# A rest product on 128 rows, and the next weights' preparation laid out over two units

## The chip, the cores and the metric

The kernel runs on one core of a Trainium2 chip. The metric is device time in microseconds (us). Before the change three runs took 1530.38, 1531.14 and 1531.47 us; their median is 1531.14 us.

## The reference

An attention block of the mLSTM kind feeds a mixture of eight experts. The attention output `x` has 3072 rows and 320 columns. The experts are dense: all of them see every row, and a matrix of weights P, made from gate logits by eight rounds of row and column normalisation, adds them up:

```python
for e in range(E):                      # E = 8
    h = np.maximum(x @ w1[e], 0.0)      # 320 -> 1024
    ye = h @ w2[e]                      # 1024 -> 320
    out += P[:, e:e + 1] * ye
```

All is in float32. The change lies in the experts 2 to 7 alone.

## The kernel before, in words

The attention and the experts 0 and 1 come first, up to about 537 us of the profiled execution. Then comes the part that the change touches. It takes the experts e = 2 to 7, the 1024 hidden columns of each in four pairs of 128-column blocks (g = 0 to 3), and the 3072 rows of x in three parts (p = 0 to 2). A *group* is one (e, g), 24 in all; a *unit* is one (e, g, p), 72 in all.

Precision. Each float32 operand is split into a high part, rounded to the type that TensorE takes (fp32r), and a low part, the remainder. ScalarE makes the high part by a copy, GpSimd or VectorE the low part by a subtraction. A product is then high x high, high x low and low x high.

A unit (`Fast.unit`, line 299) computes the two blocks of `x @ w1` for two halves of its rows by seven block products in place of eight (a Strassen-like scheme). Each product (`Fast.product`, lines 269 to 282) is four matmuls of 512 columns. Three, line 280, treat 128 of x's columns on 128 rows. The fourth, line 282, treats the "rest": x has 320 columns, and what remains of them beside 256 is stacked on 96 rows (high, low and high again, each HR = 32 rows), against three stacked pieces of the weights. The stacked x lies in DRAM (`xr`) and is loaded for every product by `rest_load` into one of twelve places in `xt` (`rest_slot`), which hold no other data by then.

The results leave PSUM in three ways: line 330 (ScalarE copies the first product), line 315 (VectorE adds a product to `tp`), and `h_parts`, which applies the ReLU and splits the hidden values: line 326 (ScalarE, high) with line 327 (VectorE, low) for the first half, and lines 322, 323 (ScalarE) with 324 (GpSimd, low) for the second. One of the two calls of line 327 in a unit reads `tp`, so both of its operands lie in SBUF; the other reads PSUM.

`Fast.second` (lines 284 to 297) multiplies the hidden values by w2: 24 matmuls of 320 columns for each half, line 297. The first half's run stands at the end of its unit, the second half's at slot 4 of the next unit. Line 158 (VectorE) adds the result into `acc`, weighted by P.

While a group is computed, the weights of the next group are prepared (`prep`, lines 1001 to 1005): `w_load` (lines 232 to 243) loads w1 and w2 in nine DMAs from SP's queue into `st` and `st2`; `w_sums` (line 248) forms four sums of blocks, in four instructions on GpSimd; `w_split` splits the main part (lines 263, 264), the rest (265, 266) and w2 (256, 257), ScalarE first and GpSimd after it. The results go into one of two sets of places, by turns of groups. There are 23 preparations inside the units, and one before them.

The order of the work is written out by hand: `at(slot, fn)` puts a piece at a slot, and the pieces are issued in the order of their slots, so a slot sets only the order on each engine and queue, not a time. A unit is 9 slots. Products stand at the slots 0 to 3 and 5 to 7, line 326 on `tp` behind slot 5.6, lines 322 to 324 at 7.7 and 7.8, the first half's second matmuls at 8. In the old plan the preparation stands in unit p = 1: the load at slot 0.9, the sums at 4.0, the splits at 5.0 and 5.1. The `rest_load` of a product is planned 9 slots before it; it waits until the product that held its place twelve products ago is done.

Of the kernel before, what the change touches and what calls it, by code (L numbers as in the profile page):

```python
# [16 lines left out]
def f32(ap):  # L17
    return ap.bitcast(F32)
# [3 lines left out]
def mlstm_moe_kernel(ctx, tc, q, k, v, i_gate, f_gate, o_gate, moe_w_gate, moe_w1, moe_w2, out):  # L22
    nc = tc.nc
# [23 lines left out]
    xt = big.tile([128, 5, NT], F32R, name="xt")  # L47
# [8 lines left out]
    late = {}  # L56
# [111 lines left out]
    HR = DR // 2  # L168
    RX = [(0, 0), 1, 2, 0, 3, (1, 1), (1, 0)]
    SLOTS = [(4, 0), (4, 1), (4, 2), (4, 3), (0, 1), (2, 1), (0, 3), (2, 3), (4, 4), (0, 5), (2, 5), (4, 5)]  # L170

    def rest_slot(n):
        k, b = SLOTS[n % len(SLOTS)]
        return xt[0:3 * HR, k, b * 512:(b + 1) * 512]

    def rest_load(n):
        nc.sync.dma_start(f32(rest_slot(n)), late["xr"][n // 7 % 3, n % 7])

    def rest_raw():
        for i, x in enumerate(RX):  # L180
# [43 lines left out]
    class Fast:  # L224
# [25 lines left out]
        def w_split(self, e, g, x):  # L250
            k = (e * NG + g) % 2
            w1 = wz[:, 3072 + 2688 * k:3072 + 2688 * (k + 1)]
            w2 = h0[:, 0:1280] if k == 0 else wz[:, 8448:9728]
            if x:
                r = late["st2"]
                nc.scalar.copy(w2[:, 0:640], r)
                nc.gpsimd.tensor_sub(w2[:, 640:1280], r, f32(w2[:, 0:640]))
                self.w[e, g] = (w1.rearrange("p (s a f) -> p s a f", s=3, f=128),
                                w2.rearrange("p (s a d) -> p s a d", s=2, a=2))
                return  # L260
            n = 7 * 128
            main, rest = (late["st"][:, m * 1024:m * 1024 + n] for m in range(2))
            nc.scalar.copy(w1[:, 0:n], main)
            nc.gpsimd.tensor_sub(w1[:, n:2 * n], main, f32(w1[:, 0:n]))
            nc.scalar.copy(w1[0:3 * HR, 2 * n:3 * n], rest[0:3 * HR])
            nc.gpsimd.tensor_sub(w1[2 * HR:3 * HR, 2 * n:3 * n], rest[2 * HR:3 * HR], f32(w1[2 * HR:3 * HR, 2 * n:3 * n]))


        def product(self, ps, e, g, p, i, w, start):
            w1 = self.w[e, g][0]  # L270
            xs = late["xs"]
            x = RX[i]
            if isinstance(x, tuple):
                k, half = x
                col = slice((2 * p + half) * 512, (2 * p + half + 1) * 512)
                hi, lo = xt[:, k, col], xt[:, k + 2, col]
            else:
                hi, lo = xs[:, p, x, 0, :], xs[:, p, x, 1, :]
            for j, (s, m) in enumerate(((0, hi), (0, lo), (1, hi))):
                nc.tensor.matmul(ps, w1[:, s, w, :], m, start=start and j == 0, stop=False, skip_group_check=True)  # L280
            n = ((e - 2) * NG + g) * 21 + p * 7 + i
            nc.tensor.matmul(ps, w1[0:3 * HR, 2, w, :], rest_slot(n), start=False, stop=True, skip_group_check=True)  # L282

        def second(self, e, g, p, half, ys, blocks, tiles_outer):

# [107 lines left out]
    def attention_phase():  # L393
# [464 lines left out]
        def at(slot, fn, *args):  # L858
            plan.setdefault(slot, []).append((fn, args))
# [126 lines left out]
        x = x0  # L986
# [11 lines left out]

        fast = Fast(moe.ps_y)

        def prep(x, e, g):
            at(x, fast.w_load, e, g)
            at(x + 3.1, fast.w_sums, e, g)
            at(x + 4.1, fast.w_split, e, g, 0)
            at(x + 4.2, fast.w_split, e, g, 1)

        todo = [(e, g) for e in range(2, E) for g in range(NG)]
        prep(x - 12, *todo[0])
        for i, (e, g) in enumerate(todo):
            for p in range(3):  # L1010
                if p == 1 and i + 1 < len(todo):
                    prep(x + 0.9, *todo[i + 1])
                items, rest = fast.unit(e, g, p)
                for slot, fn in items:
                    at(x + slot, fn)
                for j, slot in enumerate((0, 1, 2, 3, 5, 6, 7)):
                    at(x + slot - 9, rest_load, (i * 3 + p) * 7 + j)
                at(x + 4, tail.pop())
                tail.append(rest)
                x += 9  # L1020
# [7 lines left out]
    def sinkhorn(late):  # L1028
# [41 lines left out]
        return [top, top_row, top_all] + [rows, columns] * 8  # L1070

    attention_phase()


# [26 lines left out]
```

## Time and profile before

| | |
|---|---|
| median of three runs | 1531.14 us |
| profiled execution's own time | 1532.71 us |
| its span, first to last instruction | 1531.0 us |
| TensorE matmul busy | 1469.6 us (96%) |
| VectorE / ScalarE / GpSimd busy | 994.2 / 647.5 / 696.8 us |
| granted TensorE clock, mean | 0.997 of full speed (2.4 GHz) |
| the part that the change touches, from the first product | 537.6 to 1531.0 us |

Engines are named PE (TensorE's matmuls), PEld (its weight loads), DVE (VectorE), ACT (ScalarE), POOL (GpSimd) and SP (the queue that issues DMAs). L297 is line 297 of the kernel. Busy time of an engine that nobody waits for costs nothing, so the waits and the order of time count for more than the shares.

### The profile page before, as it was taken

To read this page: it belongs to the slowest core of one execution; us is meant where nothing else is said; L and a number is where in the kernel's file an instruction comes from. 1 tells how busy PE (TensorE), PEld (TensorE's weight loads), DVE (VectorE), ACT (ScalarE), POOL (GpSimd) and SP (SyncE) were. 2 spreads that over 40 slices of the span, in tenths; PEclk is the share of its full clock that TensorE was granted. 3 is DMA by queue.
4 is the path that set the end of the run, shared out by engine and by line. 5 is a ranking of instruction groups with operands and counts; after the bars stand their busy time and mean duration, and the time that the engine had idled before them with its cause. 6 is when DMAs were issued, how large, how long until landed. Compare 5 with 4: busy or idle time off the path is not lost.

```text
span 1531.0 us, 25744 instructions
## 1 busy us (share of the span) xinstructions
PE 1469.6 (96%) x9367; PEld 1344.2 (88%) x9367; DVE 994.2 (65%) x1814; ACT 647.5 (42%) x1298; POOL 696.8 (46%) x677
## 2 busy tenths in 40 slices
PE   2699999998999999999999999999999999999999
PEld 1699989997999989888998988889888899988988
DVE  4688788867332366666666666666666666666666
ACT  4677767732432233333333333333333333333332
POOL 5776767633445534443333334444344443333341
PEclk9999999999999999999999999999999999999999
DMA  9999989914211144444444343434444344443424
GB/s 193 225 186 204 202 179 200 195 40 140 64 45 46 52 128 122 124 114 129 120 124 122 117 128 107 120 113 123 125 119 127 114 127 122 122 124 114 129 83 140
DMA packets 292292, 195.43 MB, mean 128 GB/s; under 512 B 165220, under 2 KB 236164, under 8 KB 292164
## 3 DMA queue, kind: packets, MB, share of 16 engines
q1 hardware_dynamic: 291876, 193.48, 49.3%
q8 instruction: 74, 1.21, 0.3%
q14 instruction: 54, 0.44, 0.1%
q10 hardware_dynamic: 288, 0.30, 0.1%
HBM read 157.44 MB, written 11.88 MB: 111 GB/s over the span
## 4 chain that ended last, share of the span: by engine, by line
PE 88%; DVE 6%; DMA 3%; ACT 1%; SPq 1%; POOL 1%; issue 1%; POOLq 0%; DVEq 0%; ACTq 0%
PE py L297 32%; PE ph L116 11%; PE py L146 11%; PE psD L280 7%; PE psC L280 5%; PE psA L280 5%; PE psB L280 3%; DVE wz L327 3%; PE psD L282 2%; PE psA L282 2%; PE psC L282 2%; PE pss L618 1%; PE pyy L650 1%; PE psB L282 1%; DVE tp L315 1%; PE pyy L652 1%
## 5 line engine op out<-in xcount | busy, mean ns | idle before, releaser
L158 DVE SCALAR_TENSOR_TENSOR acc<-py,logits,acc 128x320 f32<-128x320 f32 x624 | 320.4, 548 | 217.1 <-PE py L297 189.5
L324 POOL TENSOR_TENSOR wz<-tp,wz 128x512 fp32r<-128x512 f32 x144 | 184.6, 1295 | 583.3 <-ACT wz L323 583.3
L297 PE MATMUL py<-h,wz 128*128 128x320 f32 x1728 | 268.4, 310 | 3.8 <-DVE wz L327 3.8
L297 PE MATMUL py<-wz 128*128 128x320 f32 x1728 | 268.2, 310 | 3.8 <-DVE wz L327 3.6
L297 PEld LDWEIGHTS py<-h,wz 128*128 128x128 f32 x1728 | 259.6, 188 | 12.9 <-DVE wz L327 7.0
L297 PEld LDWEIGHTS py<-wz 128*128 128x128 f32 x1728 | 259.5, 188 | 12.9 <-DVE wz L327 6.5
L326 ACT ACTIVATE wz<-tp 128x512 fp32r<-128x512 f32 x72 | 45.5, 632 | 419.1 <-DVE tp L315 419.1
L116 PE MATMUL ph<-xt,wz 128*128 128x256 f32 (+1 forms) x960 | 160.8, 311 | 0.0
L116 PEld LDWEIGHTS ph<-xt,wz 128*128 128x128 f32 x960 | 136.9, 193 | 6.7
L315 DVE TENSOR_TENSOR tp<-psD,tp 128x512 f32<-128x512 f32 x144 | 99.6, 692 | 39.7 <-PE psD L282 39.4
L280 PE MATMUL psD<-xs,wz 128*128 128x512 f32 x432 | 123.3, 393 | 0.0
L280 PE MATMUL psA<-xt,wz 128*128 128x512 f32 x432 | 123.3, 393 | 0.0
L315 DVE TENSOR_TENSOR tp<-psC,tp 128x512 f32<-128x512 f32 x144 | 98.9, 687 | 16.4 <-PE psC L282 15.7
L327 DVE SCALAR_TENSOR_TENSOR wz<-tp,wz 128x512 fp32r<-128x512 f32 x72 | 76.8, 1067 | 50.3 <-ACT wz L326 50.3
L146 PE MATMUL py<-wz,h 128*128 128x320 f32 x576 | 104.9, 317 | 0.0
L323 ACT CAST wz<-tp 128x512 fp32r<-128x512 f32 x144 | 89.3, 620 | 9.8
L322 ACT ACTIVATE tp<-tp 128x512 f32<-128x512 f32 x144 | 90.1, 626 | 6.2 <-DVE tp L315 6.2
L633 POOL TENSOR_TENSOR pl<-w,ph 128x512 fp32r<-128x512 f32 x48 | 63.7, 1328 | 61.0 <-ACT ph L632 61.0
L280 PEld LDWEIGHTS psD<-xs,wz 128*128 128x128 f32 x432 | 78.4, 188 | 12.0
L280 PEld LDWEIGHTS psA<-xt,wz 128*128 128x128 f32 x432 | 78.4, 188 | 12.0
L330 ACT COPY tp<-psA 128x512 f32<-128x512 f32 x72 | 42.3, 587 | 109.7 <-PE psA L282 109.7
L146 PEld LDWEIGHTS py<-wz,h 128*128 128x128 f32 x576 | 86.0, 190 | 0.9
(181 smaller groups left out, 2656.9 us busy)
## 6 DMA issues: line engine op xcount, KB each, us to landing
xt<-xr SPq DMA_DIRECT2D x504, 192.0 KB
w<-gd SPq DMA_DIRECT2D x24, 512.0 KB
st<-in_moe_w_dram SPq DMA_DIRECT2D x24, 320.0 KB
st<-in_moe_w_dram SPq DMA_DIRECT2D x56, 128.0 KB
st<-in_moe_w_dram SPq DMA_DIRECT2D x160, 32.0 KB
kn<-in_k_dram SPq DMA_DIRECT2D x24, 160.0 KB
qb<-qk SPq DMA_DIRECT2D x24, 160.0 KB
kb<-qk SPq DMA_DIRECT2D x24, 160.0 KB
```

Of the source, the lines that this page charges most:

```text
L116: nc.tensor.matmul(ph[:, a, :], w[:, kw, :], xt[:, kx, cols], start=i == 0, stop=i == len(seq) - 1)
L146: nc.tensor.matmul(ys[j][:, 0:DM], h[:, 0, j * 128:(j + 1) * 128], w, start=first and i == 0, stop=last and i == 2)
L158: nc.vector.scalar_tensor_tensor(a, y, logits[:, t, e:e + 1], a, op0=ALU.mult, op1=ALU.add)
L280: nc.tensor.matmul(ps, w1[:, s, w, :], m, start=start and j == 0, stop=False, skip_group_check=True)
L282: nc.tensor.matmul(ps, w1[0:3 * HR, 2, w, :], rest_slot(n), start=False, stop=True, skip_group_check=True)
L297: nc.tensor.matmul(ys[j][:, 0:DM], h[:, j * 128:(j + 1) * 128], w, start=i == 0, stop=i == 5)
L315: add = lambda slot, o, x, n: do(slot, lambda: nc.vector.tensor_add(tp(o), d[n], tp(x)))
L322: do(slot, lambda: nc.scalar.activation(tp(x), tp(x), AF.Relu))
L323: do(slot, lambda: nc.scalar.copy(hh, tp(x)))
L324: do(slot, lambda: nc.gpsimd.tensor_sub(hl, tp(x), f32(hh)))
L327: do(slot + 0.05, lambda: nc.vector.scalar_tensor_tensor(hl, src(), 0.0, f32(hh), op0=ALU.max, op1=ALU.subtract))
L633: nc.gpsimd.tensor_sub(flat(pl), p, f32(flat(ph)))
```

## The change

- The rest's matmul takes 128 rows. The 32 rows added are zero on both sides: twelve places in `xt` and the rows 96 to 128 of the rest's part in `st` are cleared once by GpSimd; ScalarE's copy of the rest (line 265) takes 128 rows. The DMA still brings 96 rows.
- The split is cut in three, main (0), rest (1) and w2 (2). Counted in slots of the group, that is from the start of unit p = 0: the load moves from 9.9 to 4.9, the sums from 13.0 to 8.0, the main split from 14.0 to 9.75, the rest's from 14.0 to 18.0 and w2's from 14.1 to 18.1. Slot 9 begins p = 1, slot 18 begins p = 2.
- The first group's preparation, 12 slots before its unit, keeps its order (`REST` is 0), with the clears before and between its parts.

```diff
     def rest_slot(n):
         k, b = SLOTS[n % len(SLOTS)]
-        return xt[0:3 * HR, k, b * 512:(b + 1) * 512]
+        return xt[:, k, b * 512:(b + 1) * 512]
 
     def rest_load(n):
-        nc.sync.dma_start(f32(rest_slot(n)), late["xr"][n // 7 % 3, n % 7])
+        to = f32(rest_slot(n))
+        if n < len(SLOTS):
+            nc.gpsimd.memset(to[3 * HR:128], 0.0)
+        nc.sync.dma_start(to[0:3 * HR], late["xr"][n // 7 % 3, n % 7])
...
-            if x:
+            if x == 2:
...
-            nc.scalar.copy(w1[:, 0:n], main)
-            nc.gpsimd.tensor_sub(w1[:, n:2 * n], main, f32(w1[:, 0:n]))
-            nc.scalar.copy(w1[0:3 * HR, 2 * n:3 * n], rest[0:3 * HR])
+            if x == 0:
+                nc.scalar.copy(w1[:, 0:n], main)
+                nc.gpsimd.tensor_sub(w1[:, n:2 * n], main, f32(w1[:, 0:n]))
+                return
+            nc.scalar.copy(w1[:, 2 * n:3 * n], rest)
...
-            nc.tensor.matmul(ps, w1[0:3 * HR, 2, w, :], rest_slot(n), start=False, stop=True, skip_group_check=True)
+            nc.tensor.matmul(ps, w1[:, 2, w, :], rest_slot(n), start=False, stop=True, skip_group_check=True)
...
-        def prep(x, e, g):
+        def prep(x, e, g, REST=9):
             at(x, fast.w_load, e, g)
             at(x + 3.1, fast.w_sums, e, g)
-            at(x + 4.1, fast.w_split, e, g, 0)
-            at(x + 4.2, fast.w_split, e, g, 1)
-
+            at(x + 4.1 + REST / 12, fast.w_split, e, g, 0)
+            at(x + 4.1 + REST, fast.w_split, e, g, 1)
+            at(x + 4.2 + REST, fast.w_split, e, g, 2)
+
+        LOAD = 4.9
         todo = [(e, g) for e in range(2, E) for g in range(NG)]
-        prep(x - 12, *todo[0])
+        at(x - 12, lambda: nc.gpsimd.memset(late["st"][3 * HR:128, 1024:1920], 0.0))
+        prep(x - 12, *todo[0], 0)
         for i, (e, g) in enumerate(todo):
             for p in range(3):
-                if p == 1 and i + 1 < len(todo):
-                    prep(x + 0.9, *todo[i + 1])
+                if p == 0 and i + 1 < len(todo):
+                    prep(x + LOAD, *todo[i + 1])
```

## Rows read from the trace of the kernel before

**Rows 1.** The page's first line: span and instructions.
```profile
span 1531.0 us, 25744 instructions
```

**Rows 2.** Waits of TensorE's weight loads, 538 to 1531: total us, times, longest.
```profile
PEld py L297 <- DVE wz L327: 13.4, 23, 0.6
```

**Rows 3.** Timeline of TensorE: start us, us, instructions, count [idle before <-releaser].
```profile
618.16 0.86 PE L280 MATMUL psA<-xt,wz 128*128 128x512 f32 x3
...
631.68 0.86 PE L280 MATMUL psA<-xt,wz 128*128 128x512 f32 x3
...
632.61 0.86 PE L280 MATMUL psB<-xs,wz 128*128 128x512 f32 x3
633.31 0.39 PE L282 MATMUL psB<-xt,wz 96*128 96x512 f32 x1
...
635.39 3.68 PE L297 MATMUL py<-h,wz 128*128 128x320 f32 x24
638.91 0.86 PE L280 MATMUL psD<-xs,wz 128*128 128x512 f32 x3
...
641.69 1.34 PE L297 MATMUL py<-h,wz 128*128 128x320 f32 x8
643.37 2.61 PE L297 MATMUL py<-h,wz 128*128 128x320 f32 x16 [0.34 <-DVE wz L327]
645.81 0.86 PE L280 MATMUL psA<-xt,wz 128*128 128x512 f32 x3
```

**Rows 4.** VectorE: line 327 by itself (ns min/median/max), then two rows of its timeline.
```profile
L327 DVE SCALAR_TENSOR_TENSOR wz<-tp,wz x72: 691/692/1886, 545.7 to 1519.5; 128x512 fp32r<-128x512 f32 x72
...
633.81 0.69 DVE L315 TENSOR_TENSOR tp<-psB,tp 128x512 f32<-128x512 f32 x1 [0.43 <-PE psB L282]
...
641.43 1.89 DVE L327 SCALAR_TENSOR_TENSOR wz<-tp,wz 128x512 fp32r<-128x512 f32 x1 [0.70 <-ACT wz L326]
```

**Rows 5.** Timeline of GpSimd through the same unit.
```profile
630.26 2.55 POOL L324 TENSOR_TENSOR wz<-tp,wz 128x512 fp32r<-128x512 f32 x2 [10.98 <-ACT wz L323]
632.77 2.96 POOL L248 TENSOR_TENSOR st<-st 128x256 f32<-128x256 f32 x4
636.78 2.14 POOL L264 TENSOR_TENSOR wz<-st,wz 128x896 fp32r<-128x896 f32 x1 [1.05 <-ACT wz L263]
...
641.19 1.57 POOL L257 TENSOR_TENSOR wz<-st,wz 128x640 fp32r<-128x640 f32 x1
```

**Rows 6.** Timeline of ScalarE through the same unit.
```profile
632.81 0.59 ACT L330 COPY tp<-psA 128x512 f32<-128x512 f32 x1 [1.39 <-PE psA L282]
635.76 0.94 ACT L263 CAST wz<-st 128x896 fp32r<-128x896 f32 x1 [2.36 <-POOL st L248]
636.61 0.94 ACT L265 CAST wz<-st 96x896 fp32r<-96x896 f32 x1
637.45 0.72 ACT L256 CAST wz<-st 128x640 fp32r<-128x640 f32 x1
```

**Rows 7.** Timeline of TensorE in expert 1: L116, 128 rows by 512 columns.
```profile
431.67 2.00 PE L116 MATMUL ph<-xt,xs 128*128 128x512 f32 x8
433.51 0.74 PE L146 MATMUL py<-xs,wz 128*128 128x320 f32 x4
...
511.65 1.07 PE L116 MATMUL ph<-xt,wz 128*128 128x512 f32 x4
512.56 0.60 PE L146 MATMUL py<-wz 128*128 128x320 f32 x3
```

**Rows 8.** Timeline of SP's queue: the first of the nine weight loads.
```profile
621.53 0.39 SPq L236 DMA_DIRECT2D st<-in_moe_w_dram  x1
```

**Rows 9.** Groups by line on GpSimd: the widest clear (busy us, mean ns, idle before).
```profile
L434 POOL MEMSET acc<- 96x768 f32 x1 | 0.7, 735 | 0.0
```

**Rows 10.** Timelines of TensorE and GpSimd at the first unit.
```profile
537.64 0.86 PE L280 MATMUL psA<-xt,wz 128*128 128x512 f32 x3
...
547.94 2.54 POOL L324 TENSOR_TENSOR wz<-tp,wz 128x512 fp32r<-128x512 f32 x2 [20.03 <-ACT wz L323]
```

## The prediction

> **What bounds the kernel now.** I read the page's first lines, then the waits of TensorE, then its timeline through one group of three units, then the other engines in the same stretch. TensorE's instructions fill the span [rows 1], so only two things can shorten it: a gap in TensorE's stream, or a shorter step from one matmul to the next. The waits show one recurring gap: the weight loads of L297 wait for VectorE's L327 23 times, 13.4 us in all, never over 0.6 us [rows 2]. The timeline shows where. The unit from 618.16 to 631.68 takes 13.52 us; the next, from 631.68 to 645.81, takes 14.13 us, and in it the 24 matmuls of L297 fall into 8 and 16, because the second block's low half in `wz` is late [rows 3]. That is the middle unit (p = 1) of a group. A group is one (e, g), there are 24, and 23 of them prepare a successor: 23 waits, 23 preparations.
>
> Why L327 is late is read off VectorE and GpSimd together. L327 on `tp` takes 691 ns at least, 692 in the median and 1886 at most over its 72 calls; the long one of this group runs from 641.43 for 1.89 us, starting as ScalarE releases it [rows 4]. GpSimd then has L257 in hand, from 641.19 to 642.76 [rows 5]. So VectorE's instruction starts on time and ends 0.56 us after GpSimd's. It reads both operands from SBUF. The L315 beside it read one operand from PSUM and keep 0.69 us. The present burst on GpSimd is sums (L248), L264, L266, L257, back to back from 632.77 to 642.76, and its last piece is what meets L327.
>
> **The change part by part: the moved splits.** The sums stay where they ran. The old plan has them at slot 4 of unit p = 1, the new one at slot 8 of p = 0, but GpSimd takes both behind the same two L324, that is at 632.77 [rows 5]. L263 and L264 keep their place too: L263 is now planned at slot 0.75, behind L330, and still waits for the sums. L264 then runs from 636.78 to 638.92, which is 2.5 us before L327 at 641.43 [rows 4, 5]. L266 and L257 move to the start of p = 2, behind the two L324 of p = 1. In an undisturbed unit the L324 end 1.13 us after the next unit's start (630.26 + 2.55 = 632.81 against 631.68). By the old burst L266 and L257 end 642.76 - 638.92 = 3.84 us after what stands before them, so they would end 1.13 + 3.84 = 5.0 us into p = 2. L327 starts 641.43 - 631.68 = 9.75 us into a unit. The pause is missed by 4.8 us on the right side, and every L327 should take 0.69 us.
>
> The gain per group is the difference of the two units, 14.13 - 13.52 = 0.61 us [rows 3], times 23 = 14.0 us. The wait row gives 13.4 [rows 2]. I take the middle, **13.7 us**; the ends are 13.4 and 14.0.
>
> What is late next? On ScalarE, L265 and L256 now stand ahead of L330 at the start of p = 2. Its idle time there is 1.39 us, and the two copies take 638.17 - 636.61 = 1.56 us [rows 6], so L330 starts about 0.17 us late and ends at about 633.57 on the clock of the unit shown. VectorE's L315 on `psB`, which reads its result, starts only at 633.81 because of the product itself [rows 4]. That leaves 0.24 us, so I cost it at nothing; without that cover the delay would be 0.17 us on VectorE, which TensorE does not meet before bank D is taken again, 638.91 [rows 3]. Rows 96 to 128 in L265 add partitions, not elements per partition: 96x896 and 128x896 are both 0.94 us [rows 6].
>
> On SP the nine loads of `w_load` move ahead of four `rest_load`: the last one that they follow is released not by the third product of p = 0 but by the last but one of the group before. Now they start at 621.53, about 11.2 us before the sums at 632.77, and the sums do not wait [rows 5, 8]. Earlier they have more time. They need `st` and `st2` free, which L257 gives 5.0 us into p = 2, while the release comes with the sixth product, ended 640.76 - 631.68 = 9.1 us into a unit [rows 3]: 4 us to spare. The `rest_load` behind them are asked for twelve products ahead of use. Cost: nothing.
>
> The clears are twelve of 32x512 and one of 32x896 on GpSimd, once. The widest clear in the trace, 96x768, took 0.735 us [rows 9]; with that as upper bound they are at most 9.6 us, and at the lower end nothing. GpSimd is idle for 20.03 us before its first L324 at 547.94 [rows 10]. Of these clears at most three precede the first weights' splits, 2.2 us, and the splits ended at 527.91, while the first product starts at 537.64 [rows 10]. Hidden. If a clear were held behind a read of `xt`, the splits have 9.7 us less these 2.2.
>
> **The 128 rows.** No matmul is added or dropped, so only the step between starts counts. In the unit shown sixteen matmuls of the products take 635.39 - 631.68 = 3.71 us and twelve take 641.69 - 638.91 = 2.78 us: 6.49 us for 28 [rows 3]. In L116 all matmuls are 128 rows by 512 columns, and eight of them take 433.51 - 431.67 = 1.84 us, 0.230 each [rows 7]; 28 would take 6.44. The difference is 0.05 us a unit, times 72 units = **3.6 us** gained. Bounds: the last four of such a run start within 512.56 - 511.65 = 0.91 us, 0.2275 each [rows 7]; if the whole run settled there, 28 take 6.37 and the gain is 0.12 x 72 = 8.6 us. On the other side, three 128-row steps inside a product took 633.31 - 632.61 = 0.70 us, 0.2333 each [rows 3]; if the fourth did the same, 28 take 6.53 and 0.04 x 72 = 2.9 us are lost. I take 3.6, since the eight-matmul run is the nearest row that has no change of rows in it.
>
> A rule of the Trainium skill speaks against this term. "TensorE: Matmul & The Clock Gate", section "Part 2: What happens when you issue a matmul", says that a weight load's time follows its columns and that the number of rows does not matter. By that the 128 rows give nothing, the sum is 13.7 and the time 1517.4, which is the first rival below; by the rows it is 17.3. The trace here neither bears it out nor refutes it: the runs with 96 rows differ from those without by the 0.05 us a unit, and they also differ in other things.
>
> **Sum.** 13.7 + 3.6 = 17.3 us off the span of 1531.0 us gives 1513.7. The profiled execution's own time is 1.7 us above its span and 1.6 above the median of the runs shown, so the median nearly equals that span: 1531.1 - 17.3 = **1513.8 us**.
>
> **The rivals.** *The rows change nothing:* the stall goes, the products keep 6.49 us: 1531.1 - 13.7 = 1517.4. For it: the steps around a 96-row matmul (0.23) do not stand out at this resolution. Against it: L116's shorter run. *The run settles wholly:* 1531.1 - 13.7 - 8.6 = 1508.8; for it the last four of L116, against it that the first four of each run are slower and that a product changes bank, which L116 does not. *The stall has another cause,* for instance ScalarE's burst: then 1531.1 - 3.6 = 1527.5. Against it: L327 starts right at its release and is long in itself. *Slower: the pause is missed the other way.* If the sums end over 2.5 us later, L264 (2.14 us) lies under L327 of p = 1 where L257 (1.57 us) lies now. Its 0.57 us more make the stall 1.18 us, times 23 = 27.1 instead of 14.0: 13.1 lost, 3.6 gained, 1540.6. It decides where the loads of `st` land after about 635.3; against it they are issued earlier than now.
>
> **How the numbers follow.** Chances: forecast 0.43, rows change nothing 0.32, settled run 0.15, a loss by the rows (1531.1 - 13.7 + 2.9 = 1520.3) 0.03, other cause 0.04, slower 0.03. The range 1508 to 1521 holds the first four. What this kernel's measurement can tell from no change is about 0.2%, 3 us; "other cause" is split between faster and same. Faster 0.94, same 0.02, slower 0.04.
>
> **What would show it.** In the profile after: L327 on `tp` with a maximum near 0.69 us and no waits of L297 for it; all units of equal length, near 13.47 us; L266 and L257 ending about 5 us into p = 2; L330 there preceded by L265 and L256. The row term is right if sixteen matmuls of products take 3.68 us, wrong if 3.71 (nothing) or 3.64 (settled). I am wrong at the root if L327 stays long with GpSimd idle under it, or if TensorE finds a new wait in p = 2, at `psB` or at the start of a group, where the rest's weights are now finished last.

## The result and the profile after

The kernel after takes 1510.62 us in the median of four runs (1510.0 to 1512.24), the kernel before 1531.31 us in the runs beside them (1530.38 to 1533.25). The ratio is 0.9865, 95% interval [0.9848, 0.9882]: 20.7 us faster. The forecast was 1513.8.

The profiled execution after took 1510.0 us, its span is 1508.3 us. The diff moves the lines: L297 is now L302, L327 is L332, L315 is L320, L324 is L329, L330 is L335, the sums L248 are L251, and L263 to L266, L256 and L257 are L267, L268, L270, L271, L259 and L260; the products L280 and L282 are L285 and L287. First VectorE's subtraction on `tp`, min/median/max in ns, against [rows 4]:

```profile
L332 DVE SCALAR_TENSOR_TENSOR wz<-tp,wz x72: 691/692/694, 542.6 to 1496.8; 128x512 fp32r<-128x512 f32 x72
```

The maximum has fallen from 1886 ns to 694. The waits of TensorE's matmuls, and of its weight loads, over the same part, in place of [rows 2]:

```profile
PE py L302 <- DVE acc L158: 0.3, 1, 0.3
...
PEld py L302 <- issue: 0.5, 1, 0.5
```

None of the 23 waits for VectorE's subtraction is left; the one wait stands in the last unit. TensorE's timeline through the middle unit of a group and the beginning of the third, against [rows 3]:

```profile
747.90 0.85 PE L285 MATMUL psA<-xt,wz 128*128 128x512 f32 x3
...
748.83 0.85 PE L285 MATMUL psB<-xs,wz 128*128 128x512 f32 x3
...
749.74 0.84 PE L285 MATMUL psC<-xs,wz 128*128 128x512 f32 x3
...
750.65 0.84 PE L285 MATMUL psD<-xs,wz 128*128 128x512 f32 x3
...
751.55 3.68 PE L302 MATMUL py<-wz 128*128 128x320 f32 x24
755.07 0.86 PE L285 MATMUL psD<-xs,wz 128*128 128x512 f32 x3
...
757.82 3.69 PE L302 MATMUL py<-wz 128*128 128x320 f32 x24
761.34 0.85 PE L285 MATMUL psA<-xt,wz 128*128 128x512 f32 x3
...
774.78 0.85 PE L285 MATMUL psA<-xt,wz 128*128 128x512 f32 x3
```

Both units take 13.44 us (747.90, 761.34, 774.78) where they took 14.13 and 13.53, and the 24 matmuls of L302 are one piece. The products are shorter too: sixteen matmuls 3.65 us, twelve 2.75, against 3.71 and 2.78. Of products that stand one behind the other, the first still takes 0.93 us, the following ones 0.91, 0.91 and 0.90; before, all four took 0.92 or 0.93.

Where the 20.7 us come from is read from the start of the first unit to that of the last, in the kernel before ([rows 10] has its first unit) and then in the kernel after:

```profile
1509.72 0.86 PE L280 MATMUL psA<-xt,wz 128*128 128x512 f32 x3
```

```profile
534.62 0.86 PE L285 MATMUL psA<-xt,wz 128*128 128x512 f32 x3
...
1487.10 0.86 PE L285 MATMUL psA<-xt,wz 128*128 128x512 f32 x3
```

The kernel before takes 972.1 us, the kernel after 952.5. That is 19.6 us in 71 units: 23 stalls of 0.59 us (13.5) and 71 times 0.086 us (6.1). The two profiled executions differ by 22.7 us: besides the 19.6, 3.0 lie ahead of the first product (537.64 against 534.62) and 0.1 in the last unit. That start scatters from 534.2 to 538.6 us over the profiles of before, after and the ten experiments, by no order of theirs, so the 1.1 us that the medians have beyond 19.6 are put down to this scatter, which is argued and not shown. In all twelve profiles the granted clock of TensorE is the full 2.4 GHz from 381 us to the start of the last unit, so the units compare like with like.

GpSimd through the same units, then ScalarE at the start of the third, against [rows 5, 6]:

```profile
746.48 2.55 POOL L329 TENSOR_TENSOR wz<-tp,wz 128x512 fp32r<-128x512 f32 x2 [10.89 <-ACT wz L328]
748.99 2.94 POOL L251 TENSOR_TENSOR st<-st 128x256 f32<-128x256 f32 x4
752.98 2.14 POOL L268 TENSOR_TENSOR wz<-st,wz 128x896 fp32r<-128x896 f32 x1 [1.05 <-ACT wz L267]
759.87 2.56 POOL L329 TENSOR_TENSOR wz<-tp,wz 128x512 fp32r<-128x512 f32 x2 [4.75 <-ACT wz L328]
762.51 2.13 POOL L271 TENSOR_TENSOR wz<-st,wz 32x896 fp32r<-32x896 f32 x1
764.71 1.58 POOL L260 TENSOR_TENSOR h<-st,h 128x640 fp32r<-128x640 f32 x1
```

```profile
760.88 0.94 ACT L270 CAST wz<-st 128x896 fp32r<-128x896 f32 x1
761.72 0.72 ACT L259 CAST h<-st 128x640 fp32r<-128x640 f32 x1
762.47 0.59 ACT L335 COPY tp<-psA 128x512 f32<-128x512 f32 x1
```

The sums start 1.09 us into the middle unit, as before; L268 ends at 755.12, 2.5 us before VectorE's L332 (757.58); L260 ends 4.95 us into the third unit, whose L332 starts at 771.02, 9.68 us into it. ScalarE has its two copies done at 762.44, and L335 starts 1.13 us into the unit, as it did.

### The profile page after: what moved, and what is told of

The parts are those of the page before. It is cut to its first block, busy times and chain, and to the rows that moved or that the text cites. A ratio compares the mean times of both kernels' runs of the same rounds, so it can differ in the third digit from the quotient of the medians.

```text
span 1508.3 us, 25793 instructions
## 1 busy us (share of the span) xinstructions
PE 1452.6 (96%) x9367; PEld 1338.2 (89%) x9367; DVE 966.9 (64%) x1814; ACT 645.4 (43%) x1298; POOL 702.7 (47%) x690
## 4 chain that ended last, share of the span: by engine, by line
PE 93%; DMA 3%; DVE 2%; SPq 1%; POOL 1%; issue 0%; ACT 0%; ACTq 0%; POOLq 0%; DVEq 0%
PE py L302 34%; PE ph L116 11%; PE py L146 11%; PE psA L285 7%; PE psD L285 7%; PE psC L285 7%; PE psB L285 3%; PE psA L287 2%; PE psD L287 2%; PE psC L287 2%; PE pss L623 1%; DMA acc<-in_moe_w_dram 1%; PE pyy L655 1%; PE psB L287 1%; PE pyy L657 1%; PE pu L699 1%
## 5 line engine op out<-in xcount | busy, mean ns | idle before, releaser
L329 POOL TENSOR_TENSOR wz<-tp,wz 128x512 fp32r<-128x512 f32 x144 | 183.9, 1298 | 556.7 <-ACT wz L328 556.7
L302 PE MATMUL py<-wz 128*128 128x320 f32 x1728 | 265.1, 309 | 0.3 <-DVE acc L158 0.3
L302 PE MATMUL py<-h,wz 128*128 128x320 f32 x1728 | 265.1, 309 | 0.0
L302 PEld LDWEIGHTS py<-wz 128*128 128x128 f32 x1728 | 259.1, 188 | 6.4 <-issue 0.5
L302 PEld LDWEIGHTS py<-h,wz 128*128 128x128 f32 x1728 | 259.2, 188 | 5.9
L116 PE MATMUL ph<-xt,wz 128*128 128x256 f32 (+1 forms) x960 | 159.7, 309 | 0.0
L116 PEld LDWEIGHTS ph<-xt,wz 128*128 128x128 f32 x960 | 135.8, 191 | 6.7
L320 DVE TENSOR_TENSOR tp<-psD,tp 128x512 f32<-128x512 f32 x144 | 99.6, 691 | 38.6 <-PE psD L287 38.2
L285 PE MATMUL psD<-xs,wz 128*128 128x512 f32 x432 | 122.3, 391 | 0.0
L285 PE MATMUL psA<-xt,wz 128*128 128x512 f32 x432 | 122.2, 391 | 0.0
L320 DVE TENSOR_TENSOR tp<-psC,tp 128x512 f32<-128x512 f32 x144 | 99.0, 687 | 15.0 <-PE psC L287 14.4
L328 ACT CAST wz<-tp 128x512 fp32r<-128x512 f32 x144 | 89.4, 621 | 9.9
L327 ACT ACTIVATE tp<-tp 128x512 f32<-128x512 f32 x144 | 90.0, 625 | 0.0
L285 PEld LDWEIGHTS psD<-xs,wz 128*128 128x128 f32 x432 | 78.2, 188 | 11.4
L285 PEld LDWEIGHTS psA<-xt,wz 128*128 128x128 f32 x432 | 78.2, 188 | 11.4
L332 DVE SCALAR_TENSOR_TENSOR wz<-tp,wz 128x512 fp32r<-128x512 f32 x72 | 49.8, 692 | 50.3 <-ACT wz L331 50.3
L128 DVE SCALAR_TENSOR_TENSOR wz<-ph,wz 128x512 fp32r<-128x512 f32 x48 | 33.0, 688 | 75.7 <-ACT wz L127 75.7
```

Of the source, the lines that this page charges most:

```text
L116: nc.tensor.matmul(ph[:, a, :], w[:, kw, :], xt[:, kx, cols], start=i == 0, stop=i == len(seq) - 1)
L302: nc.tensor.matmul(ys[j][:, 0:DM], h[:, j * 128:(j + 1) * 128], w, start=i == 0, stop=i == 5)
L320: add = lambda slot, o, x, n: do(slot, lambda: nc.vector.tensor_add(tp(o), d[n], tp(x)))
L327: do(slot, lambda: nc.scalar.activation(tp(x), tp(x), AF.Relu))
L328: do(slot, lambda: nc.scalar.copy(hh, tp(x)))
L329: do(slot, lambda: nc.gpsimd.tensor_sub(hl, tp(x), f32(hh)))
```

## Experiments

### The two parts, each alone

The 128 rows alone are the kernel after with the plan of before:

```diff
-            at(x + 4.1 + REST / 12, fast.w_split, e, g, 0)
-            at(x + 4.1 + REST, fast.w_split, e, g, 1)
-            at(x + 4.2 + REST, fast.w_split, e, g, 2)
+            at(x + 4.1, fast.w_split, e, g, 0)
+            at(x + 4.1, fast.w_split, e, g, 1)
+            at(x + 4.2, fast.w_split, e, g, 2)
...
-                if p == 0 and i + 1 < len(todo):
-                    prep(x + LOAD, *todo[i + 1])
+                if p == 1 and i + 1 < len(todo):
+                    prep(x + 0.9, *todo[i + 1])
```

> The 128 rows alone, on the old plan of the preparation. Theory: a change of the row count (96 to 128) between two products slows the next five matmuls, and without it a run of products settles at 0.227 us a matmul after its first five. So all three units shrink by 0.086 us, 6.2 us in 72 units, about 1525; the middle unit keeps its stall of 0.59 us and L297's waits for L327 stay near 13.4 us. Rival: it is the change of PSUM bank from product to product that slows them; then the products keep their steps and the time stays near 1531. The rule that rows do not matter gives 1531 too.

Measured: 1526.55 us, ratio 0.9975 [0.9965, 0.9985], so 3.8 us faster by the ratio (4.9 between the medians) where 6.2 were expected. TensorE's timeline in that run, one middle unit between two others:

```profile
737.76 0.85 PE L285 MATMUL psA<-xt,wz 128*128 128x512 f32 x3
...
751.20 0.85 PE L285 MATMUL psA<-xt,wz 128*128 128x512 f32 x3
...
761.12 1.34 PE L302 MATMUL py<-wz 128*128 128x320 f32 x8
762.87 2.61 PE L302 MATMUL py<-wz 128*128 128x320 f32 x16 [0.42 <-DVE wz L332]
765.32 0.86 PE L285 MATMUL psA<-xt,wz 128*128 128x512 f32 x3
...
778.76 0.63 PE L285 MATMUL psA<-xt,wz 128*128 128x512 f32 x2
```

The units beside the middle one take 13.44 us, so the saving is there in full, and PSUM's bank still changes from product to product: the rival is out. The middle unit takes 14.12, no less than before. Its end is set by GpSimd's burst, not by TensorE: L260 ends 11.07 us into this unit (762.27), as L257 did before (11.08). What the products save there, the stall takes back (the weight loads wait 15.6 us in place of 13.4). Over the 71 units the two kernels differ by 4.0 us.

The plan alone is the kernel after with `0:3 * HR` rows in `rest_slot`, the copy and the matmul, and without clears:

> The new plan of the preparation alone, with 96 rows and no clears. Theory: the 23 stalls go, every unit takes 13.526 us, 13.5 us in all, about 1517.7. Rival: the two parts help each other (the stall goes only with shorter products, or the rest's place costs something of its own); then this and the run with the rows alone do not add up to the 20.7 us of both.

Measured: 1518.6 us, ratio 0.9915 [0.9901, 0.9929]; all three units of a group take 13.527 us in the median, the subtraction 693 ns at most, and the 71 units 13.45 us less. So the stall goes without any help from the rows. But 3.96 + 13.45 = 17.4 is 2.2 short of 19.6: the 23 middle units give their 0.09 us only when the stall is gone. The parts help each other in this one way.

### Which piece of the burst

w2's split alone moved to the third unit, 96 rows, all else as before (`w_split` cut in three as in the change; the calls in `prep`):

```diff
             at(x + 4.1, fast.w_split, e, g, 0)
-            at(x + 4.2, fast.w_split, e, g, 1)
+            at(x + 4.1, fast.w_split, e, g, 1)
+            at(x + (4.2 if REST == 0 else 8.2), fast.w_split, e, g, 2)
```

> The kernel before, with w2's split alone (L256, L257) moved to the start of unit p = 2; load, sums, main and rest stay. Theory: only the GpSimd instruction that is in hand when L327 starts matters; L266 then ends at 641.1 by the clock of the unit shown and L327 starts at 641.4, so all 23 stalls go and the time is that of the whole new plan, about 1517.7. Rival: the burst as a whole delays the chain (ScalarE's three copies, or a port held across the burst); then part of the stall stays, some 0.2 to 0.4 us a group, 1522 to 1527.

Measured: 1518.17 us, ratio 0.9912 [0.9899, 0.9926], and the units are 13.527 us each. VectorE's subtraction in that run:

```profile
L329 DVE SCALAR_TENSOR_TENSOR wz<-tp,wz x72: 691/691/693, 544.6 to 1504.9; 128x512 fp32r<-128x512 f32 x72
```

One piece, w2's split, was the whole stall. It has two instructions, ScalarE's L256 and GpSimd's L257, so this run alone does not tell them apart. The trace of before does: ScalarE was idle for 2.59 us before the L326 that releases L327.

```profile
640.76 0.63 ACT L326 ACTIVATE wz<-tp 128x512 fp32r<-128x512 f32 x1 [2.59 <-DVE tp L315]
```

So ScalarE's burst is out as the cause, and GpSimd's L257, 1.57 us long, is left.

The rest's and w2's split moved, load, sums and main split left (`x + 8.1` and `x + 8.2` for the parts 1 and 2):

> The kernel before with the rest's and w2's split moved to the start of p = 2, but load, sums and main split planned where they were, and 96 rows. Theory (as the prediction had it): GpSimd and ScalarE do the sums and the main split at the same time as under the new plan, so it equals the plan alone, about 1517.7; moving the load and the sums is worth nothing. Rival: the main split, now planned behind slot 5 and not at 0.75, comes late or the later load is late; then 0.1 us or more a group remains, over 1520.

Measured: 1517.8 us, ratio 0.9899 [0.9878, 0.9921], units of 13.527 us. Moving the load, the sums and the main split is worth nothing here, nor is moving the rest's split.

The last two pieces exchanged (part 2 at `x + 4.1`, part 1 at `x + 4.2`):

> The kernel before with the last two pieces of the burst exchanged: w2's split first, the rest's after it, so that L266 (32 partitions, 2.1 us) lies under L327 instead of L257 (128 partitions, 1.6 us) and the burst ends at the same time. Theory: the number of partitions does not matter; L327 ends about 0.55 us after L266, the stall stays 0.5 to 0.6 us a group and the time near 1531. Rival: an instruction on 32 partitions leaves room; then L327 takes 0.69 us and the time is about 1517.7.

Measured: 1530.88 us in one run, middle units of 14.01 us. GpSimd's instruction on 32 partitions, and VectorE's subtraction (L268 and L329 in that kernel):

```profile
764.01 2.13 POOL L268 TENSOR_TENSOR wz<-st,wz 32x896 fp32r<-32x896 f32 x1
```

```profile
764.92 1.77 DVE L329 SCALAR_TENSOR_TENSOR wz<-tp,wz 128x512 fp32r<-128x512 f32 x1 [0.70 <-ACT wz L328]
```

GpSimd's was in hand until 766.14, and VectorE's ended 0.55 us after that. An instruction on 32 partitions holds VectorE back as one on 128 does.

### One instruction, or the burst

The kernel before with its four sums computed twice has a longer burst, and L264 moves to where L257 was:

```diff
-            for o, x, y in ((T1, W12, W11), (T3, W22, W12), (T2, W22, T1), (T4, W21, T2)):
+            for o, x, y in ((T1, W12, W11), (T3, W22, W12), (T2, W22, T1), (T4, W21, T2)) * 2:
```

> The kernel before, its four sums computed twice: 2.96 us more on GpSimd, so that L264 (639.7 to 641.9), L266 and L257 follow each other without a pause to 645.8 and L327 (641.4) meets L264's end instead of L257. Theory: VectorE waits for the one GpSimd instruction in hand and gets in before the next; L327 then ends about 0.55 us after L264, takes 1.0 us, TensorE does not stall and the time falls to about 1517.7, though GpSimd does more. Rival: GpSimd keeps the port while it has instructions back to back; then L327 lasts to about 646.3, 4.9 us, the stall is 3.6 us a group and the time about 1600.

Measured: 1521.07 us, ratio 0.9928 [0.9913, 0.9944]: more work, and 10 us faster. GpSimd's timeline in a middle unit, then VectorE's, then ScalarE's:

```profile
761.70 2.13 POOL L264 TENSOR_TENSOR wz<-st,wz 128x896 fp32r<-128x896 f32 x1 [1.05 <-ACT wz L263]
763.91 2.46 POOL L266 TENSOR_TENSOR wz<-st,wz 32x896 fp32r<-32x896 f32 x1
```

```profile
763.65 0.73 DVE L327 SCALAR_TENSOR_TENSOR wz<-tp,wz 128x512 fp32r<-128x512 f32 x1 [0.92 <-ACT wz L326]
```

```profile
761.52 0.94 ACT L265 CAST wz<-st 96x896 fp32r<-96x896 f32 x1
762.36 0.72 ACT L256 CAST h<-st 128x640 fp32r<-128x640 f32 x1
762.99 0.63 ACT L326 ACTIVATE wz<-tp 128x512 fp32r<-128x512 f32 x1
```

VectorE's instruction gets in between L264 and L266: it ends at 764.38, 0.55 us after L264. L266, which started meanwhile, takes 2.46 us instead of 2.12, so GpSimd waits for VectorE as well. The rival by which GpSimd holds VectorE back through a whole burst is out. The 1.0 us expected of L327 did not come, because L326 now stands behind ScalarE's copies and starts 0.23 us late: L327 meets only the last 0.18 us of L264 and takes 0.73. That delay is also part of the 3.4 us to the expected 1517.7: the middle units keep 0.075 us, 1.7 us in all. The rest is not explained.

### What on GpSimd holds VectorE back

Four runs put an instruction of GpSimd under the subtraction in the units p = 0 of the kernel after, released with `tp(u2)`; its result goes to a spare place and is not used. The pieces, one run each:

```diff
+            if p == 0:
+                spare = wz[:, 10752:11264]
...
+                do(5.55, lambda: nc.gpsimd.tensor_sub(spare, tp(u2), f32(wz[:, 9728:10240])))
...
+                for _ in range(3):
+                    do(5.55, lambda: nc.gpsimd.tensor_copy(spare, tp(u2)))
...
+                do(5.55, lambda: nc.gpsimd.tensor_copy(spare[:, 0:256], tp(u2)[:, 0:256]))
+                do(5.55, lambda: nc.gpsimd.tensor_copy(spare, tp(u2)))
...
+                do(5.55, lambda: nc.gpsimd.tensor_copy(spare[:, 0:256], tp(u2)[:, 0:256]))
+                do(5.55, lambda: nc.gpsimd.memset(f32(spare), 0.0))
```

The subtraction:

> The kernel after, with one GpSimd subtraction (two operands, 128x512, 1.3 us) at the same place in each unit p = 0; its result is not used. Both theories: VectorE's subtraction starts about 0.6 us after it and ends about 0.55 us after GpSimd's end, so it takes about 1.2 us in 24 of its 72 calls; it ends at the edge of what TensorE tolerates, so stalls are 0.1 us or none. It is the control for the run with copies.

GpSimd's and VectorE's timelines in that run (1511.73 us):

```profile
745.33 1.29 POOL L347 TENSOR_TENSOR wz<-tp,wz 128x512 fp32r<-128x512 f32 x1 [7.94 <-DVE tp L320]
```

```profile
745.95 1.22 DVE L332 SCALAR_TENSOR_TENSOR wz<-tp,wz 128x512 fp32r<-128x512 f32 x1 [0.70 <-ACT wz L331]
```

VectorE's instruction takes 1.22 us and again ends 0.55 us after GpSimd's (746.62). TensorE keeps its step. Three copies:

> The kernel after, with three GpSimd copies (one operand, 128x512) in each unit p = 0, released with ScalarE's first ReLU, so that they lie under VectorE's subtraction with both operands in SBUF. They compute nothing that is used. Theory 1: any GpSimd instruction in hand holds VectorE's subtraction back; it then takes over 0.9 us in 24 of its 72 calls. Theory 2: only GpSimd instructions with two operands do; it keeps 0.69 us. Time within 3 us of the kernel after either way.

Measured: 1513.14 us. The run does not decide what it was made for: VectorE kept 694 ns at most, but the first copy ended 0.02 us before VectorE's instruction started. It showed the other side: the second copy, which started in the meantime, took 1.13 us instead of 0.62. In the next run a copy is in hand when VectorE starts:

> As the run with three copies, but a first copy of 256 columns and a second of 512, so that the second (0.61 us) begins about 0.3 us before VectorE's subtraction and is in hand when it starts. Theory 1 (any GpSimd instruction that reads SBUF holds it back): VectorE's subtraction lasts until about 0.55 us after the copy's end, 0.8 to 0.95 us in 24 of 72 calls. Theory 2 (only two operands do): it keeps 0.69 us and the copy is not stretched.

GpSimd's and VectorE's timelines in that run (1513.86 us):

```profile
747.86 0.62 POOL L348 CAST wz<-tp 128x512 fp32r<-128x512 f32 x1
```

```profile
748.04 0.98 DVE L332 SCALAR_TENSOR_TENSOR wz<-tp,wz 128x512 fp32r<-128x512 f32 x1 [0.70 <-ACT wz L331]
```

A copy, with one operand, holds VectorE back too: the subtraction ends 0.54 us after the copy. Last, the clear:

> The same with a clear of 512 columns (0.52 us, reads nothing) as the second piece. Theory 1 in its wide form (the write port is shared too, or a lock covers the whole instruction): VectorE's subtraction is held until the clear's end, 0.75 to 0.85 us. In its narrow form (reads alone collide): it keeps 0.69 us and the clear 0.52 us.

GpSimd's and VectorE's timelines in that run (1509.84 us):

```profile
743.56 0.53 POOL L348 MEMSET wz<- 128x512 f32 x1
```

```profile
743.73 0.69 DVE L332 SCALAR_TENSOR_TENSOR wz<-tp,wz 128x512 fp32r<-128x512 f32 x1 [0.70 <-ACT wz L331]
```

The clear lies under the instruction for 0.36 us, and VectorE's takes 0.69 us as ever; the clear's 0.53 us is close to the 0.52 of the clears of 32x512. The copy reads SBUF and writes it, the clear only writes: it is GpSimd's reading that holds VectorE back, as far as one form of each can tell.

## Why the prediction was right, point by point

- **The stall** was read rightly, in its cause, its place and its size: 13.7 us forecast, 13.5 measured in the units, and the runs that move one part alone show it by itself. Everything that was to stay in place did: the sums, the main split, the end of L260 at 4.95 us into the third unit (forecast 5.0). The burst of before was not quite back to back, as the prediction has it: GpSimd is idle for 1.05 us before L264 [rows 5]. Nothing hangs on that.
- **ScalarE** was to be 0.17 us late at L335 and was not: in this unit L328 ends 0.37 us before the next unit starts, where the row read has 0.26, the first copy starts right behind it, and the two are through as psA's product ends. The cover was not needed.
- **The clears** took 0.52 us each for 32 rows by 512 and were hidden. The one of 32x896 took 0.84, more than the 0.735 that the prediction took as a bound for each; the thirteen together, 7.1 us, stay under its 9.6. SP's queue cost nothing.
- **The 128 rows** are the term that was mis-sized: 3.6 us forecast, 6.1 measured, inside the bounds of -2.9 and 8.6. By the prediction's own sign, sixteen matmuls in 3.68 us, it failed: they take 3.65, nearer to the 3.64 of the settled run. I spread the mean of an eight-matmul run over runs of twelve and sixteen. But the slow steps stand at a run's start, and in eight matmuls they weigh more than in sixteen. The trace of before had this already: step by step, L116's eight matmuls take 231, 236, 228, 233, 231, 226, 227 and 227 ns. The sixteen of the kernel after begin with the same five, to within 1 ns, and then stay at 226 or 227. With 96 rows every product repeated slow steps: 231 to 233, 236, 228 and 230 ns in the median. The Trainium skill ("TensorE: Matmul & The Clock Gate", section "Part 2: What happens when you issue a matmul") has the time of a weight load follow its columns, whatever its rows. The trace agrees for the load by itself, 188 ns at 96 and at 128 rows. That the rows then give nothing, as the prediction puts the rule, does not hold: they changed a unit by 0.086 us. The time by that rule, 1517.4, is about what the plan alone gives (1518.6).
- **The rival of the settled run** (1508.8) came closer to the measured 1510.62 than the forecast (1513.8) did. What the prediction held against it is half right: a run's first steps are slower, but the change of bank from product to product does not keep a run from settling.
- **What I had not seen:** the two terms are not a plain sum. The rows are worth 4.0 us on the old plan and 6.1 on the new one. The order in which I added them, the stall first and the rows on top, happened to be right for the whole. That was luck and not reasoning.
- **The slower rival** had a real mechanism: in the run with the sums doubled L327 does meet L264, though only its last 0.18 us, and in the one with the rest last a long meeting stalls TensorE. The price hangs on where GpSimd's instruction ends, for VectorE's ends 0.55 us after it. On the new plan L268, the former L264, ends 2.5 us before L332 starts.

The gain is 20.7 us where 17.3 were forecast. Of the 3.4 between them, 2.5 are the row term (6.1 - 3.6) and 1.1 are not found in the 71 units; the stall was 0.2 too large. Left open is why a change of rows, or of 320 to 512 columns, slows the matmuls behind it; no run separates the weights' side from the moving side. With both parts in, TensorE waits once in the whole part, so no run here points to a version that is faster than the kernel after.

## What to carry to other kernels

When one call of a repeated instruction is far longer than the others though it starts at its release, look at what another engine has in hand at that moment, and move that one piece; which other pieces move with it may not matter. A saving on an engine that waits for another one in the same stretch is not paid out until the wait is gone, so parts measured alone can add up to less than the whole. A step's price is better read from the settled part of a long run and from its start apart than from the mean of a short one.

## What the runs showed of the hardware

- VectorE's 128x512 subtraction with both operands in SBUF waits for the GpSimd instruction in hand when that one reads SBUF, with one operand or two, on 32 partitions or 128, and ends 0.54 to 0.56 us after it. It does not wait for the GpSimd instructions queued behind, and these wait for VectorE in turn (2.46 us for 2.12, 1.13 for 0.62). A clear of 128x512 on GpSimd left VectorE's subtraction at 0.69 us. VectorE's additions with one operand in PSUM (L315) took 0.69 us at most, under GpSimd's sums too.
- One matmul of 96 rows among three of 128 kept each run of products from settling: 0.92 to 0.93 us for four matmuls in place of 0.90 to 0.91.
